# A new order of emission for a fused attention and gated convolution kernel on one core

## The chip, the core and the metric

The kernel runs on one core of a Trainium2 chip. The metric is the device time in microseconds (us) of one execution. TensorE (PE in the profile) multiplies matrices, with its weight loads shown as PEld; VectorE is DVE, ScalarE is ACT, GpSimd is POOL, SyncE is SP, which here only starts transfers.

## The reference, cut to what matters

For each of 8 batches `x` is 8 heads x 512 rows x 64, and `state` 8 heads x 32 rows x 64. The rows of `x` and the rows of `state` read each other by softmax attention, and what both read goes, as 544 rows of 512 features, through a gated convolution network:

```python
scores = scale * np.matmul(x, state.transpose(0, 1, 3, 2))       # softmax over the 32 state rows -> a
xread = np.matmul(a, state)
scores2 = scale * np.matmul(state, x.transpose(0, 1, 3, 2))      # softmax over the 512 rows -> a2
sread = np.matmul(a2, x)
h = np.maximum(x @ w_in, 0.0)                                    # x: xread and sread, heads side by side
conv_out += conv_w[k][None, None, :] * hp[:, k:k + S, :]         # 3 taps along the rows
gate = 1.0 / (1.0 + np.exp(-conv_out))
return (h * gate @ w_out).astype(np.float32)
```

## The kernel before

The kernel is one program of some 1,660 small operations. Each is recorded by `add(engine, kind, function, reads, writes)` and has a number by the place at which it was recorded. `Plan.order` then emits them in the order of the list `ORDER`: a number is an operation, `-n` puts n filling multiplications (`fill`, L215, on tile `idle`, whose result nobody reads) on PE, and a `v` behind a number puts an operation that ACT does by default onto DVE. Each engine, and each queue of transfers, takes its operations in the order in which the list gives them; waits are made from the data and the buffers. So the list is the schedule, and nothing else decides it. Eight PSUM banks (`PSUM = dict(ps=8)`) are handed round among all that PE writes.

What PE does, per batch b:

- **scores** (L310 into `ps_s`; for batch 0 in two halves, L320): 8 multiplications that use 64 rows and 32 columns of the array each.
- **flips** (L355 into `ps_t`, 4 transposes of 128 columns), **reads** (L368 into `ps_r`, 32 multiplications on 32 columns each), and **read flips** (L379 into `ps_f`, one transpose): the state rows' own softmax and what they read.
- **state products** (L548 into `ps_u`, for half hf of the hidden features; for batch 0 in blocks of 1, 1, 2 and 4 times 128 features, L567): state times `w_in`, 8 multiplications of the same shape as the scores. ACT and DVE split the result into two parts, `u0` (high) and `u1` (low).
- **hidden** (L630 into `ps_h`, 6 multiplications of 128x128 by 512 columns each; batch 0 has 4 of 256 columns, L637) and **projections** (L705 into `acc`, 3 multiplications of 512 columns for each of 4 row groups c and 8 feature blocks f; the very first ones L713).
- **state tokens** (L615 into `ps_hs`, 4 of 128 columns) and their projection (`acc_t`), and at the end of batch 0 one leftover projection (`acc_c`).

I call L630, L637, L705 and L713 the wide multiplications and all the others small groups. Batch 0's softmax over the state rows is done with PE's help: flip of the scores (L488 into `ps_x`), maximum (DVE, L492), shift (L498 into `ps_s`), exponential (ACT, L508 into `p`), sum (L512), reciprocal (DVE), spread (L498 into `ps_x`), division (DVE, L523), all in two halves q.

Between hidden and projection stand, for each of 64 steps, a relu on ACT (L200, or DVE), a first tap on ACT (L194), two taps on DVE (L673, L678), tanh on ACT (L682), the gate on DVE (L687), and a split into a high part (ACT, L205) and a low part (DVE, L208). The weights come as raw words and are rounded on the way in by ACT (L243 into `hc`, L246) and DVE (L249, L252, L260). All large loads stand in SP's queue; ACT's queue holds the first part of the state (`st`, the part of batch 0) and the convolution's weights.

Names that the change and the prediction use: tile numbers behind a name tell copies apart, and `e` is the exponential of a score half (L346), which the flips read.

Of the kernel before, what the change touches and what calls it, by code (L numbers as in the profile page):

```python
# [58 lines left out]
0 98 99 100 101 102 103 120 -9 123 121 125 -3 124 -1 142 143 126 2 -2 150 3 127 5 20 4 144 151 128 6 -1 152 132 145  # L59
146 130 7 21 461 14 23 15 17 22 147 16 148 24 18 25 153 19 154 155 133 8 9 462 10 135 11 149 32 467 33 463 12 156 34  # L60
468 469 26 489 28 136 27 530 35 1 13 36 129 464 157 29 37 38 131 189 30 465 466 39 190 40 41 531 532 31 192 42 200 534
199 191 43 515 490 44 535 491 45 47 193 46 202 203 48 205 516 493 204 517 49 536 206 502 503 210 504 519v 494 537 520
211 122 137 212 470 471 472 538 521 159 158 208 161 213 506 545 575 546 138 162 214 163 134 507 560 207 56 50 51 139
209 169 495 140 201 215 52 170 533 496 576 590 164 179 53 508 54 497 141 172 55 165 180 522 216 62 57 59 217 167 64 63
65 539 66 523 67 591 547 166 168 173 518 58 218 561 500 219 562 240 241 509 243 60 160 510 171 174 499 244 61 501 246
514 513 505 512 524 525 540 245 526 251 175 108 247 176 252 177 249 254 181 109 529 528 74 68 69 178 70 563 255 511 71
182 72 297 298 541 300 250 73 183 242 256 110 111 527 549 548 301 592 542 543 248 544 550 253 257 338 339 75 258 577
551 259 184 552 260 185 553 564 579 302 341 342 492 343 565 77 186 76 78 580 566 291 281 289 285 187 286 290 555 86 80
421 567 282 82 287 295 581 188 556 296 81 292 568 87 83 283 582 595 288 569 84 79 380 379 89 583 293 85 554 88 112 593
612 113 92 642 613 284 578 616 596 498 597 657 614 627 114 643 628 557 294 194 631 598 570 629 197 382 195 106 617 90  # L70
115 599 571 91 594 1516 558 559 574 572 573 198 196 349 600 618 116 1654 585 584 586 104 93 383 95 646 94 117 107 96
1655 658 660 619 615 645 620 97 647 601 384 118 1656 602 1657 119 105 672 717 687 589 588 702 621 644 1658 673 703 648
632 587 649 603 604 606 608 609 420 605 630 1659 650 235 230 633 236 634 659 350 233 1660 220 238 610 635 221 622 636
718 651 705 674 688 222 352 624 625 704 223 353 661 231 239 234 237 637 423 626 640 224 225 652 226 655 641 227 232
228 662 607 611 229 639 706 691 690 656 623 638 1661 721 676v 663 654 707 677 664 665 424 678 666 340 425 719 689 692
667 708 679 693 722 426 694 695 755 740 741 709 756 758 696 710 261 653 770 670 815 669 671 720 680 845 711 846 681
427 675 800 785 697 390 682 684 685 385 757 743 759 700 771 686 668 774 344 683 723 744 724 760 712 761 698 699 725
713 849 772 745 345 762 726 773 786 775 763 764 742 347 715 816 348 727 262 746 714 747 729 776 777 734 728 263 765
789 264 730 830 778 748 701 735 1662 831 788 749 819 817 716 732 801 733 265 271 328 346 850 266 790 272 351 354 847
# [874 lines left out]
```

## Time and profile before

| what | value |
| --- | --- |
| time, median of 3 runs | 356.75 us (355.89 to 357.86) |
| span of the profiled execution | 354.1 us |
| PE busy, share of the span | 348.6 us, 98% |
| DVE busy | 316.1 us, 89% |
| ACT busy | 256.1 us, 72% |
| granted TensorE clock | 1.00 |
| HBM read and written | 25.71 MB and 8.91 MB |

The profiled execution's own time is not listed apart from its span; the median of the timed runs lies 2.65 us above the span. The page's 40 slices show PE at 90% or more from the second slice (8.9 us) on, DVE at 90% or more in the slices 2 to 25 (to about 221 us) and less behind them, and ACT at 90% or more up to some 70 us. A row of the timeline gives the start of a run of like instructions, its busy time, engine, line, tiles, shape and count; a multiplication of 32-bit floats is counted twice, one of the split parts (512 columns, L630 and L705) once. The busy times of neighbours overlap, so what a group costs is read from its start to the next start.

### The profile page before, as it was taken

What the parts mean: (1) busy time and instruction counts of PE and PEld (TensorE: products, weight loads), DVE (VectorE), ACT (ScalarE), POOL (GpSimd) and SP (SyncE); (2) the same over time, 40 slices, a digit from 0 to 9 for tenths busy, and PEclk for the clock granted to TensorE, in tenths of its full rate; (3) what the DMA queues carried; (4) which work ended last, traced back from release to release, by engine and by line L of the source; (5) the groups of instructions that cost most, each with busy time, mean ns of one, the idle gap of its engine ahead of it and who ended that gap; (6) DMA issues with size and microseconds to landing.
All of it is one profiled execution on the core that took longest, in us unless ns stands there. A gap on an engine that the chain in (4) does not pass through costs nothing.

```text
span 354.1 us, 6694 instructions
## 1 busy us (share of the span) xinstructions
PE 348.6 (98%) x2538; PEld 271.8 (77%) x2538; DVE 316.1 (89%) x563; ACT 256.1 (72%) x560; POOL 29.4 (8%) x90
## 2 busy tenths in 40 slices
PE   7999999999999999999999999999999999999995
PEld 6766758876788868878789887878788868888884
DVE  1999999999999999999999999987799898889950
ACT  3999999998777997859856657774745447548642
POOL 1000000010000000100000300042201001113000
PEclk9999999999999999999999999999999999999999
DMA  7989998201600033030400000001200011000205
GB/s 255 396 309 377 328 357 302 62 1 50 219 0 2 0 127 142 3 119 32 180 30 2 0 31 31 30 3 60 89 2 0 0 71 65 2 2 0 74 33 176
DMA packets 13584, 35.06 MB, mean 99 GB/s; under 512 B 1520, under 2 KB 4720, under 8 KB 12528
## 3 DMA queue, kind: packets, MB, share of 16 engines
q1 hardware_dynamic: 12976, 34.28, 27.1%
q8 instruction: 20, 0.33, 0.4%
q10 hardware_dynamic: 576, 0.35, 0.3%
q14 instruction: 12, 0.10, 0.1%
HBM read 25.71 MB, written 8.91 MB: 98 GB/s over the span
## 4 chain that ended last, share of the span: by engine, by line
PE 97%; DMA 2%; ACT 0%; SPq 0%; issue 0%
PE acc L705 47%; PE ps_h L630 22%; PE ps_h L637 4%; PE ps_hs L615 4%; PE ps_u L548 4%; PE acc_t L705 3%; PE ps_r L368 2%; PE ps_t L355 2%; PE ps_s L310 2%; DMA xt<-xT 2%; PE acc_c L705 2%; PE acc L713 2%; PE ps_u L567 1%; PE ps_s L498 1%; PE ps_x L498 1%; PE ps_x L512 1%
## 5 line engine op out<-in xcount | busy, mean ns | idle before, releaser
L705 PE MATMUL acc<-wo,g 128*128 128x512 f32 x726 | 177.0, 393 | 0.0
L705 PEld LDWEIGHTS acc<-wo,g 128*128 128x128 f32 x726 | 134.7, 188 | 32.8 <-issue 1.7
L630 PE MATMUL ps_h<-a,u 128*128 128x512 f32 x336 | 83.2, 391 | 0.0
L630 PEld LDWEIGHTS ps_h<-a,u 128*128 128x128 f32 x336 | 62.7, 188 | 13.1
L682 ACT ACTIVATE t<-t 128x512 f32<-128x512 f32 x64 | 39.9, 630 | 14.5 <-DVE t L678 14.3
L673 DVE SCALAR_TENSOR_TENSOR t<-h,cw,t 128x511 f32<-128x511 f32 x64 | 47.1, 742 | 1.6 <-ACT t L194 1.5
L678 DVE SCALAR_TENSOR_TENSOR t<-h,cw,t 128x512 f32<-128x512 f32 (+1 forms) x64 | 46.8, 745 | 0.6
L205 ACT ACTIVATE g<-t 128x512 fp32r<-128x512 f32 (+1 forms) x62 | 37.5, 615 | 11.0 <-DVE t L687 5.5
L687 DVE SCALAR_TENSOR_TENSOR t<-t,h 128x512 f32<-128x512 f32 (+1 forms) x64 | 42.4, 667 | 2.3 <-ACT t L682 2.2
L208 DVE TENSOR_TENSOR g<-t,g 128x512 fp32r<-128x512 f32 (+1 forms) x62 | 41.3, 671 | 3.5 <-ACT g L205 3.1
L194 ACT ACTIVATE t<-h,cw 128x512 f32<-128x512 f32 x52 | 36.9, 723 | 4.3 <-DVE h L202 3.0
L200 ACT ACTIVATE h<-ps_h 128x512 f32<-128x512 f32 x56 | 33.3, 596 | 9.3 <-PE ps_h L630 6.1
L648 POOL COPY h<-hs 128x1 f32<-128x1 f32 x40 | 14.2, 376 | 129.2 <-ACT sr L383 66.3
L205 ACT ACTIVATE u<-ps_u 128x512 fp32r<-128x512 f32 x28 | 16.2, 596 | 8.5 <-PE ps_u L548 8.5
L719 ACT ACTIVATE o<-acc 128x512 f32<-128x512 f32 (+1 forms) x30 | 15.8, 544 | 8.5 <-PE acc L705 8.3
L648 POOL COPY hs<-h 128x1 f32<-128x1 f32 x40 | 13.6, 361 | 97.6 <-ACT h L200 80.9
L208 DVE TENSOR_TENSOR u<-ps_u,u 128x512 fp32r<-128x512 f32 x28 | 18.6, 682 | 2.5 <-ACT u L205 2.5
L615 PEld LDWEIGHTS ps_hs<-sr,wi 128*128 128x128 f32 x128 | 14.8, 192 | 1.1 <-ACT t L194 0.8
L637 PE MATMUL ps_h<-p,u 128*128 128x256 f32 x64 | 15.3, 386 | 0.0
L615 PE MATMUL ps_hs<-sr,wi 128*128 128x128 f32 x128 | 15.0, 276 | 0.0
L548 PE MATMUL ps_u<-wi,st 64*32 64x512 f32 x224 | 14.3, 597 | 0.0
L637 PEld LDWEIGHTS ps_h<-p,u 128*128 128x128 f32 x64 | 11.6, 190 | 3.3 <-DVE hc L249 0.8
(99 smaller groups left out, 400.3 us busy)
## 6 DMA issues: line engine op xcount, KB each, us to landing
xt<-xT SPq DMA_DIRECT2D x16, 512.0 KB, 7.7
xx<-xn SPq DMA_DIRECT2D x8, 1024.0 KB, 5.9
out<-o SPq DMA_DIRECT2D x27, 256.0 KB, 2.1
raw<-w_in SPq DMA_DIRECT2D x8, 512.0 KB, 7.6
raw<-w_out SPq DMA_DIRECT2D x8, 512.0 KB, 7.4
out<-o SPq DMA_DIRECT2D x6, 128.0 KB, 1.8
out<-o_t SPq DMA_DIRECT2D x8, 64.0 KB, 1.7
st<-stT SPq DMA_DIRECT2D x1, 448.0 KB, 10.2
```

The source lines that it names most:

```text
L194: A.activation(dst, src, AF.Copy, scale=scale)
L200: A.activation(dst, src, AF.Relu, scale=0.5)
L205: A.activation(hi, src, AF.Copy)
L208: engine.tensor_tensor(lo, src, hi.bitcast(F32), op=ALU.subtract)
L615: PE.matmul(ps_hs[m, f][:, :NT], wi[:, k, f * P:(f + 1) * P], sr[m][:, k, :], start=(k == 0), stop=(k == NK - 1))
L630: PE.matmul(ps_h[i], u[j][:, g, fs], a[k][:, g, :], start=(n == 0), stop=(n == 3 * NG - 1))
L637: PE.matmul(ps_h[f][:, q * HS:(q + 1) * HS], us[0, f // 4][0][:, g, f % 4 * P:(f % 4 + 1) * P], half_of(pa[0], q)[:, g, :], start=(g == 0) ...
L673: V.scalar_tensor_tensor(t[:, 1:], h[:, :S - 1], cw[:, f, 0:1], t[:, 1:], op0=ALU.mult, op1=ALU.add)
L678: V.scalar_tensor_tensor(t[:, :n], h[:, 1:n + 1], cw[:, f, 2:3], t[:, :n], op0=ALU.mult, op1=ALU.add)
L682: A.activation(tt[i], tt[i], AF.Tanh, scale=0.25)
L687: V.scalar_tensor_tensor(tt[i][:, :n], tt[i][:, :n], 1.0, hd[i][:, :n], op0=ALU.add, op1=ALU.mult)
L705: PE.matmul(acc, g[j][:, cs], wo[:, k, f, :], start=(f == 0 and n == 0), stop=(f == NF - 1 and n == 2))
```

## The change

Only the list `ORDER` is another one: the same operations, in another order. Both lists hold 16 fills: before, 9, 3, 1, 2 and 1 in the first microseconds; now 7, 3, 1, 1, 1 and 1 there and two single ones among batch 0's hidden products. By a `v`, DVE takes 25 operations before and 24 now: 12 and then 11 first taps (L196), 8 and then 7 relus (L202), and 5 evacuations of sums at the end (L721; four of 512 columns, one of 256) and then 6 (one of 512, five of 256). One line of the list, before and now:

```diff
@@ ORDER
-0 98 99 100 101 102 103 120 -9 123 121 125 -3 124 -1 142 143 126 2 -2 150 3 127 5 20 4 144 151 128 6 -1 152 132 145
+0 98 99 100 -2 101 -3 102 103 -2 120 123 125 -1 121 -2 142 2 124 126 3 143 144 145 14 -1 127 132 5 150 151 -1 4 146 6
...
```

In ACT's queue the first part of the state is the first transfer in both orders. In SP's queue the rest of the state (`st`, L894) stands 9th before and 11th now, with one load of `x` and one of `w_in` more ahead of it.

The first place is PE in the first microseconds, batch 0's softmax by PE (`ps_x` the flipped scores and later the spread sums, `ps_s` the scores that are shifted, `heads` the sum). Before, the two flips stand ahead of both shifts:

```order
L488 MATMUL ps_x_141<-ident,at_112 128x128 x4
L215 MATMUL idle<-zeros 128x128 x2
L488 MATMUL ps_x_154<-ident,at_112 128x128 x4
L498 MATMUL ps_s_0_0_113<-eight,m_0_146 32x128 x8
L498 MATMUL ps_s_0_1_114<-eight,m_0_146 32x128 x8
L215 MATMUL idle<-zeros 128x128
L498 MATMUL ps_s_1_0_130<-eight,m_1_183 32x128 x8
L498 MATMUL ps_s_1_1_131<-eight,m_1_183 32x128 x8
L512 MATMUL ps_x_141<-heads,p_208 128x4 x4
L355 MATMUL ps_t_215<-ident,e_0_185 128x128 x4
```

Now, on the same engine, behind the first flip (which has moved ahead of the second half of the scores, the eight L321 rows just before these):

```order
L499 MATMUL ps_s_0_0_111<-eight,m_0_149 32x128 x8
L499 MATMUL ps_s_0_1_112<-eight,m_0_149 32x128 x8
L216 MATMUL idle<-zeros 128x128
L489 MATMUL ps_x_178<-ident,at_110 128x128 x4
L216 MATMUL idle<-zeros 128x128
L513 MATMUL ps_x_128<-heads,p_167 128x4 x4
L499 MATMUL ps_s_1_0_135<-eight,m_1_183 32x128 x8
L499 MATMUL ps_s_1_1_136<-eight,m_1_183 32x128 x8
L499 MATMUL ps_x_128<-ident,s_0_211 32x128 x16
L216 MATMUL idle<-zeros 128x128
```

The first half's flip, shift and sum have moved ahead of the second half's; the flip of `e_0` has moved behind the spread.

The second place is PE among batch 0's hidden products (`ps_h`, each `x2` is one half). Before, behind the second batch's scores (last row of them first):

```order
L310 MATMUL ps_s_1_412<-xt_388,st 32x512
L637 MATMUL ps_h_396<-p_208,u_0_223 128x256 x2
L637 MATMUL ps_h_438<-p_208,u_0_223 128x256 x4
L368 MATMUL ps_r_457<-xx_455,e2t_359 32x64 x16
L368 MATMUL ps_r_457<-xx_455,e2t_331 32x64 x16
L567 MATMUL ps_u_3_0_493<-wi,st 32x512
```

Now, at the same place:

```order
L311 MATMUL ps_s_1_393<-xt_312,st 32x512
L638 MATMUL ps_h_344<-p_167,u_0_241 128x256 x2
L638 MATMUL ps_h_429<-p_167,u_0_241 128x256 x4
L216 MATMUL idle<-zeros 128x128
L638 MATMUL ps_h_447<-p_167,u_0_241 128x256 x4
L369 MATMUL ps_r_464<-xx_445,e2t_347 32x64 x16
L369 MATMUL ps_r_464<-xx_445,e2t_342 32x64 x16
L568 MATMUL ps_u_3_0_500<-wi,st 32x512
```

Four products more stand behind the scores, and a fill between them; a second such fill stands 23 rows further on.

The third place is PE and DVE where batch 2's projections begin (`ps_t` the flips of batch 7, `acc` the sums). PE before, from the last row of a state product on; the second flip stands alone among wide multiplications 48 rows further on:

```order
L548 MATMUL ps_u_0_1_1683<-wi,st 32x512
L368 MATMUL ps_r_1701<-xx_1424,e2t_1607 32x64 x16
L368 MATMUL ps_r_1701<-xx_1424,e2t_1339 32x64 x16
L355 MATMUL ps_t_1740<-ident,e_14_1508 128x128 x4
L705 MATMUL acc_3_1358<-wo,g_15_1586 128x512
```

PE now, from the last two rows of a state product on, which itself follows the read:

```order
L549 MATMUL ps_u_0_0_1727<-wi,st 32x512
L549 MATMUL ps_u_0_1_1728<-wi,st 32x512
L356 MATMUL ps_t_1744<-ident,e_14_1721 128x128 x4
L356 MATMUL ps_t_1764<-ident,e_15_1673 128x128 x4
L706 MATMUL acc_1_1328<-wo,g_15_1607 128x512
L706 MATMUL acc_1_1328<-wo,g_15_1606 128x512 x2
```

DVE before, around the low half of a state product (`u1`) whose bank the sum `acc_3` of batch 2 takes over:

```order
L454 TENSOR_TENSOR af_3_1463<-af_3_1463,s1_3_1666 128x1024
L678 SCALAR_TENSOR_TENSOR t_23_1577<-h_23_1503,cw_78,t_23_1577 128x512
L457 STREAM_TRANSPOSE at_3_737<-af_3_1463 128x1024
L208 TENSOR_TENSOR g1_18_1750<-t_18_1553,g0_18_1749 128x512
L208 TENSOR_TENSOR u1_3_0_1669<-ps_u_3_0_0_1670,u0_3_0_1668 128x512
L673 SCALAR_TENSOR_TENSOR t_21_1655<-h_21_1605,cw_78,t_21_1655 128x511
```

DVE now, around the low half whose bank `acc_3` takes over in the new order:

```order
L458 STREAM_TRANSPOSE at_3_683<-af_3_1533 128x1024
L674 SCALAR_TENSOR_TENSOR t_20_1717<-h_20_1481,cw_78,t_20_1717 128x511
L197 TENSOR_SCALAR t_22_1761<-h_22_1660,cw_78 128x512
L209 TENSOR_TENSOR u1_4_0_1726<-ps_u_4_0_1_1728,u0_4_0_1725 128x512
L209 TENSOR_TENSOR a1_3_1759<-at_3_683,a0_3_1758 128x1024
```

The read, the state product and both flips stand in one stretch now, and the bank comes from another state product, that of batch 4, which stands 231st on DVE; the one before stood 229th.

## Rows read from the trace of the kernel before

**Rows 1.** The page, sections 1 and 4: busy time by engine; the chain's shares.

```profile
PE 348.6 (98%) x2538; PEld 271.8 (77%) x2538; DVE 316.1 (89%) x563; ACT 256.1 (72%) x560; POOL 29.4 (8%) x90
...
PE 97%; DMA 2%; ACT 0%; SPq 0%; issue 0%
```

**Rows 2.** Busy time by engine in a stretch; stretch, length, engines, clock, DMA share, GB/s.

```profile
20.00:140.00 120.00, 119.96 (x1040) 88.83 (x1040) 117.64 (x207) 106.19 (x247) 2.40 (x4) 1.00 0.46 163
```

**Rows 3.** Timeline of PE, a lone state product; start, busy us, engine, line, what, count.

```profile
233.53 2.88 PE L705 MATMUL acc<-wo,g 128*128 128x512 f32 x12
236.34 1.09 PE L548 MATMUL ps_u<-wi,st 64*32 64x512 f32 x16
237.36 5.07 PE L705 MATMUL acc<-wo,g 128*128 128x512 f32 x21
242.27 2.88 PE L630 MATMUL ps_h<-a,u 128*128 128x512 f32 x12
244.99 0.84 PE L705 MATMUL acc<-wo,g 128*128 128x512 f32 x3
```

**Rows 4.** Timeline of PE, two state products side by side.

```profile
287.05 1.52 PE L705 MATMUL acc_t<-wo,gts 128*128 128x512 f32 x6
288.50 1.95 PE L548 MATMUL ps_u<-wi,st 64*32 64x512 f32 x32
290.38 2.33 PE L705 MATMUL acc<-wo,g 128*128 128x512 f32 x9
292.55 1.52 PE L630 MATMUL ps_h<-a,u 128*128 128x512 f32 x6
```

**Rows 5.** Timeline of PE, a lone flip, and a flip right behind a read.

```profile
120.97 0.60 PE L355 MATMUL ps_t<-ident,e 128*128 128x128 f32 x4
121.32 3.70 PE L705 MATMUL acc<-wo,g 128*128 128x512 f32 x15
124.85 1.52 PE L630 MATMUL ps_h<-a,u 128*128 128x512 f32 x6
...
130.57 0.66 PE L355 MATMUL ps_t<-ident,e 128*128 128x128 f32 x4
130.99 7.09 PE L705 MATMUL acc<-wo,g 128*128 128x512 f32 x30
137.92 0.27 PE L379 MATMUL ps_f<-ident,rr 128*128 128x128 f32 x1
```

**Rows 6.** Timeline of all engines in the first 24 us, the softmax of batch 0.

```profile
1.03 3.70 PE L215 MATMUL idle<-zeros 128*128 128x128 f32 x18 [1.03 <-DVE zeros L177]
...
5.81 0.66 ACT L194 ACTIVATE at<-ps_s 128x256 f32<-128x256 f32 x2 [0.76 <-PE ps_s L320]
...
8.09 0.60 PE L488 MATMUL ps_x<-ident,at 128*128 128x128 f32 x4
...
9.57 1.08 PE L498 MATMUL ps_s<-eight,m 128*32 128x128 f32 x32
...
10.05 0.72 ACT L346 ACTIVATE e<-at,nm 128x512 f32<-128x512 f32 x1 [0.17 <-DVE nm L340]
...
13.57 0.69 ACT L508 ACTIVATE p<-ps_s 128x256 f32<-128x256 f32 x2
...
16.36 0.77 PE L567 MATMUL ps_u<-wi,st 64*32 64x256 f32 x16
...
18.07 1.99 PE L637 MATMUL ps_h<-p,u 128*128 128x256 f32 x8
...
19.99 0.45 PE L567 MATMUL ps_u<-wi,st 64*32 64x128 f32 x16
```

**Rows 7.** The transfer of the rest of the state: its issue; size and time to landing.

```profile
6.53 0.43 SPq L894 DMA_DIRECT2D st<-stT  x1
...
st<-stT SPq DMA_DIRECT2D x1, 448.0 KB, 10.2
```

**Rows 8.** Timeline of DVE, the low half of a state product (`u1_3_0`).

```profile
134.10 0.68 DVE L208 TENSOR_TENSOR u<-ps_u,u 128x512 fp32r<-128x512 f32 x1
```

More of the change, by code (lines that the diff above doesn't have):

```diff
@@ new lines @@
+829 844 859 321 322 309 310 889 828 843 902 958 873 323 856 874 959 875 440 960 395 311 312 903 961 324 325 860 392
+1521 441 1522 922 357 358 876 923 396 842 857 858 307 326 928 890 299 891 929 930 877 739 973 943 944 945 886 313 333
+397 398 314 315 931 904 866 867 905 974 976 946 975 316 317 327 1041 962v 963 399 442 443 473 444 487 477 474 892 478
[5 rows of a table added]
+994 995 1034 359 969 984 1020 1057v 1059 408 1021 360 361 1089 1104 1060 1005 1035 1006 1071 1072 369 372 410 411 373
+370 371 1036 481 482 483 1527 1528 362 1010 1025 1040 412 1009 1050 1007 1022 1075 363 364 1037 1051 1052 365 1074 366
@@ new lines @@
+1105 1076 1529 1008 1023 1038 1061 413 367 368 1106 1058 484 1062 1090 1024 1039 988 1073 1077 1078 989 1091 414 1054
+1063 1530 1079 1124 1125v 1080 1055 1064 1154 1065 1139 1066 999 1053 1092 1107 1093 1094 1169 1170 1081 1069 1070
+1140 1143v 1095 1096 1108 1068 1109 374 1141 1127 409 377 378 1085 1155 1171 1084 1083 1110 1173 1099 1111 375 376
+1098 1113 1100 1174 1175 1176 1532 1128v 1158 1129 1533 1229 1126 1130 1199 1144 1131 1067 1534 1535 1536 1537 1132
+1133 1538 1159 1145 1082 1177 1230 1115 1122 1232 1146 1147 1097 1156 1112 1116 1117 1540 1160 1161 1114 1134 1184
@@ new lines @@
+1178 1162 1163 1541 1542 1543 1531 1539 1118v 1185 1214 1179 1148 1136 1149 1142 1157 1135 1150 1172 1544 1164 1151
+415 1215 1218 1217 1188v 1189 1186 1166 1216 1187 1200v 1201 1119 1138 1137 1153 1168 1545 1152 1546 416 1167 1182
+1219 1190 1548 1120 1549 1550 1203 418 419 1204 1551 1165 1552 1252 449 1191 1192 1205 1206 1207 1180 417 1193 1194
+1183 1220 1357 1312 1221 1222 450 1197 1253v 1553 1554 1208 1282 1358 1198 1209 1359 1202 1256 1231 1212 1313 1223
+1315 1556 1254 1257 1258 1557 1547 1558 1283v 1286v 1195 1181 1196 1255 1224 1285 1233 1259 1210 1316 1317 1287 1260
[4 rows of a table added]
@@ new lines @@
+1306 1307 1571 1264 1380 1381 1279 1263 1265 1280 1410 1576 1577 1578 1292 1585 1383 1346v 1347 1396 1579 1398 1294
+1281 1348 1296 1349 1278 1293 1364 1329 1308 1586 1587 1350 1588 1589 1590 1591 1365 458 1295 1331 1332 1333 1351 1352
+1592 1399 1321 1322 1311 1326 1580 1584 1583 1309 1411v 1582 1414v 1366 1581 1593 1310 1397 1324 1594 1595 1323 1325
+1425 1334 1335 1596 1597 1413 1598 1599 1336 1337 1341 1382 1384v 1385 1601 1386 1387 1485 1340 1400 1401 1602 1426
+1603 1455 1429 1430 1427 1604 1249 1339 1605 1606 1607 1338 1353 1367 1431 1609 1388 1389 1415 1610 1368 1354 1440
@@ L121 @@
+1412 1355 1372 1373 1402 1600 1456v 1459 1390 1428 1611 1612 1416 1369 1356 1371 1457 1417 1370 1460 1403 1404 1405
[4 rows of a table added]
+1634 1635 1636 1637 1638 1639 1484 1641 1642 1488 1643 1644 1645 1481 1646 1647 1499 1512v 1513 1496 1500 1502v 1503
+1640 1648 1649 1650 1652 1514v 1651 1501 1452 1467 1653 1482 1515 1497 1504v 1506v 1507 1505 1468 1483 1498 1508 1510
+1511 1509
 """
```

25 lines of the change are left out of this document (3 added, 22 removed), and 74 rows, old and new, of the table ORDER.

## The prediction

> **What bounds the kernel now.** I read the busy shares and the chain of waits first: PE is busy 348.6 of 354.1 us and holds 97% of the chain that ends last [rows 1]. Then the stretches: from 20 to 140 us PE has 119.96 of 120 us, so it waits for nothing there, at a granted clock of 1.00 (the 2.4 GHz level); but DVE has 117.64 of the same 120 [rows 2], so it runs with 2.36 us in hand. Behind some 220 us DVE is freer. So the time is the sum of what PE is given, plus a head of some 7 us before it is fed. A new order adds and removes no product. It can pay in three ways only: by the changes between kinds of multiplication, by an earlier first product, and by waits that it makes or spares. None has much to give.
>
> **The change part by part.** *Joins.* I price a group by starts: from the start of what stands before it to the start of what stands behind, less the wide multiplications at their own price. That price is (244.99 − 242.27)/12 = 0.2267 us [rows 3]. A lone state product: 242.27 − 233.53 = 8.74, less 33 × 0.2267 = 7.48, is 1.26 [rows 3]. Two side by side: 292.55 − 287.05 = 5.50, less 15 × 0.2267 = 3.40, is 2.10 [rows 4]. So two together save 2 × 1.26 − 2.10 = 0.42. A lone flip costs 124.85 − 120.97 = 3.88, less 15 × 0.2267 = 3.40, that is 0.48. A flip behind a read: 137.92 − 130.57 = 7.35, less 30 × 0.2267 = 6.80, is 0.55 [rows 5]; of this 0.15 belongs to the next entry into a small group (the 21 wide ones before 242.27 took 4.91 instead of 4.76 [rows 3]), which leaves 0.40. So a flip joined to a read saves 0.08, a fifth of the other.
>
> In the two orders, from the first hidden product on, small groups stand in 34 separate stretches among wide multiplications before and in 22 now (the two stretches that hold only a fill not counted). The places at which one small group touches another rise from 23 to 36. Of these 13 more, two are 64-row groups beside 64-row groups (state products, scores: 6 before, 8 now), none is a 64-row group beside a read (6 and 6), and 11 are of flips, read flips or state tokens (11 and 22). Dear joins: 2 × 0.42 = 0.84. The cheap ones lie between 0 (a read flip is one transpose, a quarter of a flip) and 0.08 each; I take 0.05, since over half are flips: 11 × 0.05 = 0.55. Sum 1.39, bounds 0.84 and 1.72. PE is the bound, so all of it counts.
>
> The rows show where the price sits: the lone state product goes 236.34 to 237.36, 1.02; the two together 288.50 to 290.38, 1.88 [rows 3, 4]. The second costs 0.86, so 0.16 is saved inside, and the rest at entry. The Trainium skill, "TensorEngine Tiling (Array Packing)", section Key Properties, says that changing the tiling mode, not just the tile, drains the engine. By that page only joins of one mode would pay, and the sum would be 0.84 instead of 1.39. The flip behind a read is of another mode, and 0.08 was saved, so the trace agrees only in part.
>
> *Fills among the hidden products.* Two of the 16 stand there now. Nine of them at the start take 3.70 (18 in the row, since each counts twice), so one is 3.70/9 = 0.41 us [rows 6]. If PE would not wait at that place, it is lost: 2 × 0.41 = 0.82. If it would wait there anyway, nothing. I take 0.82: PE did not wait there before.
>
> *The head.* Before, the flip of the first scores starts at 8.09 and its shift at 9.57, 1.48 later; the scores' copies on ACT end at 5.81 + 0.66 = 6.47 already, and between stand the second half's scores [rows 6]. Now this flip stands ahead of those, so the first half's chain can start some 1.5 us earlier. The second half still waits for its own scores, and on ACT the exponential `e` (10.05, 0.72 and 0.17 of wait), which stood ahead of the second half's `p` (13.57), now stands behind it [rows 6]: that takes 0.72 + 0.17 = 0.89 off ACT's chain to `p`. The flips of `e` stand behind and then wait some 0.2 for it, so the first hidden product (18.07) comes 0.7 earlier; bounds 0 (`p` not on the path) and 0.89. But by then a block of 128 features has been multiplied in place of the one of 256: 0.77 − 0.45 = 0.32 is only put off [rows 6]. Net 0.70 − 0.32 = 0.38, bounds −0.32 and 0.57.
>
> *The state's load.* The first part of the state is first in ACT's queue in both orders, so there the words of the change say nothing new. The rest of the state goes back in SP's queue by two loads of 512 KB. It was issued at 6.53 and landed 10.2 later, at 16.7 [rows 7]; its first use stands behind the 128 block, at 19.99 + 0.45 = 20.4 [rows 6]. With eight loads ahead of it these 10.2 make 10.2/9 = 1.1 for each place in the queue, so two places more are an estimated 2.3, and it lands at 19.0. That is ahead of its use by 1.4, so I take nothing; each further microsecond would hold up the next state product and all that follows. The loads that it lets pass come earlier, and PE waits for none of them at that time.
>
> *Places on DVE.* One first tap and one relu go back to ACT, which has room behind 70 us. The evacuations at the end are the same in kind: I take nothing. What the order does to DVE's due times is the open cost. At the first multiplication of batch 2's `acc_3`, in the run of 30 that starts at 130.99, PE needs a bank that the low half `u1_3_0` empties on DVE at 134.10 + 0.68 = 134.78 [rows 8]. In this run it is the 19th: 130.99 + 18 × 0.2267 = 135.07 [rows 5], so 0.3 of slack. Now it needs the low half of batch 4, 231st on DVE instead of 229th, while 314 wide multiplications instead of 323 are ahead of it on PE: PE comes 9 × 0.2267 = 2.04 earlier and DVE two instructions of about 0.68 later, 1.36. If DVE has no more in hand than before, PE waits 2.04 + 1.36 − 0.3 = 3.1 there; if the small groups ahead of it differ, or the 2.36 us of DVE's idle time [rows 2] lie ahead of it and close, 3.1 − 2.36 = 0.7, or nothing. A wait that is once paid moves PE back against DVE for all that follows, so such waits do not add up. I take 0.3, since before PE waited nowhere in that stretch; bounds 0 and 3.1.
>
> Sum: 1.39 − 0.82 + 0.38 − 0.30 = 0.65 faster. The span goes from 354.1 to 353.4. The median of the runs lies 2.65 above the span, so the time goes from 356.75 to **356.1**.
>
> **The rivals.** *DVE sets the pace (slower).* The place is the one above. For it: 98% of DVE's time is taken between 20 and 140 us, and nine products fewer stand ahead of the bank. Against it: PE never waited there before, and a list that puts small groups together gives DVE its inputs in larger lots, which may also come earlier. The price is 2 to 4 us of PE waits in place of the 0.3: time 356.75 − 0.95 + 2 to 4 = 357.8 to 359.8. It makes the kernel slower once the waits exceed the gain of 0.95, and measurably so from 0.95 + 1.78 = 2.7 on.
>
> *Joins of different kinds save nothing.* Then only the two dear joins pay: 0.84 − 0.82 + 0.38 = 0.40, time 356.35. For it: a read flip is a single transpose, and its place may be too short to save anything. Against it: the 0.08 of the flip behind a read, though that is a difference of two readings of 3.9 and 7.4 us. The rule on modes in the page named above would give this time.
>
> *All that is open falls well.* PE would wait at the fills anyway, the cheap joins are worth 0.08 and the head gives 0.57: 1.72 + 0.57 = 2.29 and no waits, time 354.5. For it: with the small groups among batch 0's hidden products at other places, waits may be there that were not before, and a fill in one is free. Against it: PE waited nowhere behind 20 us, and two of the three bounds would have to be met at once.
>
> *The order does not do what it says.* The joins are there in the list, but the state's load comes later than its first use, and the state product behind the 128 block waits with all behind it. A delay of 1 to 2 us beyond the 1.4 in hand gives 357.1 to 358.1. Against it: eight loads ahead took no more than 10.2 together.
>
> **How the numbers follow.** Forecast (DVE's waits below 1 us) 0.51; DVE sets the pace 0.20; joins of one kind only 0.12; all falls well 0.13; the load late 0.04. Two timings of this kernel can be told apart from about 0.5%, 1.78 us: faster is below 354.97, slower above 358.53. Faster holds most of the case in which all falls well and a little of the forecast, by the median's own scatter (355.89 to 357.86): 0.12 + 0.07 = 0.19. Slower holds some 0.6 of DVE's case and a little of the load's: 0.12 + 0.01 = 0.13. Same: 0.68. For 8 in 10 I leave out the upper part of DVE's case (0.11) and the lower part of the gain (0.08): 354.7 to 358.2.
>
> **What would show it.** *Joins:* two state products side by side cost 2.1 between their neighbours' starts, and PE's busy time falls by about 1.4 with fills and head apart. A flip joined to a read at 0.5 says that the cheap joins are nothing. *Fills:* a unit of 0.41 between hidden products with no wait beside it; a wait right behind it says that it cost nothing. *Head:* `p` of the second half some 0.9 and the first hidden product some 0.7 earlier, at 17.4; if not, `p` was not on the path. *State:* landing before 20 us. *DVE:* no idle time of PE put down to DVE between 20 and 140 us, at `acc_3` of batch 2 above all; 2 us or more of it there makes the forecast wrong on the slow side, and one large wait on the load or on ACT would do so too. A time below 354.9 would say that a join is worth about twice what I read.

## The result and the profile after

The changed kernel takes 359.49 us, median of 14 runs, against 356.78 us of 14 runs of the kernel before: a ratio of 1.0067, 95% interval 1.0048 to 1.0085. That is slower by 0.7%, outside the forecast range of 354.7 to 358.2 and on the other side of no change. One execution, the one that was profiled with the result, ran PE at half its pace to the end (708.61 us, span 706.8) and does not count in the ratio (median of the other 13: 359.24), so the profile shown here is of another execution of the same kernel, of 357.52 us, shorter than all of those 13 (358.21 to 360.62).

In every run that lists both, the time lies 1.8 us above the span (357.52 and 355.7 here). So the profile of the kernel before, with its span of 354.1, is that of its run of 355.89, the shortest of the three, and the 2.65 us of the forecast are these 1.8 and the 0.9 from that run to the median. The two profiles differ by 1.6 us of the 2.5 by which the medians differ.

First the page and the stretch from 20 to 140 us, as in [rows 1, 2]:

```profile
PE 348.4 (98%) x2538; PEld 272.3 (77%) x2538; DVE 318.8 (90%) x562; ACT 258.5 (73%) x561; POOL 30.7 (9%) x90
...
PE 66%; DVE 22%; ACT 5%; DMA 4%; issue 2%; SPq 0%; DVEq 0%; ACTq 0%
```

```profile
20.00:140.00 120.00, 118.97 (x1040) 88.47 (x1039) 118.07 (x208) 107.79 (x252) 0.78 (x2) 1.00 0.41 148
```

PE's busy time is the same to 0.2 us, but its share of the chain has fallen from 97% to 66%, and DVE has taken 22%. From 20 to 140 us PE now stands still for 1.03 us where it stood still for 0.04. What PE waited for (engine, tile and line, what it waited for; us in all, times, longest):

```profile
PE ps_s L321 <- DMA xt<-xT: 0.9, 1, 0.9
PE ps_r L369 <- DMA xx<-xn: 0.5, 1, 0.5
PE acc_t L706 <- DVE gts L209: 0.4, 1, 0.4
PE acc L706 <- DVE u L209: 0.4, 1, 0.4
```

The last three have no like in the profile of the kernel before: the load of `x` for a read, the last state tokens' gates, and the low half of a state product (`u`), which is the place of the forecast's slower rival. The wait for a load of `x` does appear in other profiles of the order of before: 0.4 us with seven fills, and 0.9 in the relieved kernel before (both below). The head, to be read against [rows 6]:

```profile
1.03 3.35 PE L216 MATMUL idle<-zeros 128*128 128x128 f32 x14 [1.03 <-DVE zeros L178]
5.26 0.67 PE L321 MATMUL ps_s<-xt,st 64*32 64x256 f32 x16 [0.87 <-DMA xt<-xT]
5.86 0.94 PE L216 MATMUL idle<-zeros 128*128 128x128 f32 x6
6.63 0.60 PE L489 MATMUL ps_x<-ident,at 128*128 128x128 f32 x4
...
12.72 1.00 SPq L895 DMA_DIRECT2D st<-stT  x1
...
12.88 0.63 ACT L509 ACTIVATE p<-ps_s 128x256 f32<-128x256 f32 x2
...
17.70 2.76 PE L638 MATMUL ps_h<-p,u 128*128 128x256 f32 x12
```

The first flip stands at 6.63 instead of 8.09, the second `p` at 12.88 instead of 13.57, the first hidden product at 17.70 instead of 18.07.

To say where time goes I use three marks that both kernels share: the start of the first, the 121st and the last (1210th) hidden product or projection, taken from the starts of single multiplications in each trace.

| profile | first | first to 121st | 121st to last |
| --- | --- | --- | --- |
| kernel before | 18.07 | 52.55 | 279.53 |
| changed kernel | 17.70 | 53.27 | 280.92 |
| without two fills | 19.36 | 53.46 | 280.95 |
| nine fills at the start | 17.84 | 53.64 | 280.85 |
| before, seven fills | 17.84 | 53.18 | 279.53 |
| three waits mended | 18.46 | 54.53 | 279.56 |
| two waits mended | 17.94 | 55.54 | 279.49 |
| relieved, after | 21.00 | 52.31 | 279.53 |
| relieved, before | 18.25 | 54.92 | 279.52 |
| reads earlier | 20.97 | 54.60 | 279.55 |
| head of before | 18.43 | 56.08 | 279.48 |
| head of after, before | 20.22 | 53.15 | 279.53 |
| fewer loads, after | 18.12 | 52.62 | 279.47 |
| fewer loads, before | 19.69 | 52.33 | 279.51 |

(The names are those of the experiments below; the kernels put together from two lists at 41 and 72 us and the joins alone are not listed; "before" behind a comma is the kernel before with that edit.) The last column repeats to 0.1 us from profile to profile, at 280.9 in the changed order and at 279.5 in the others; the first two do not. The second varies in the order of before as well (52.33 to 54.92), so a single profile says little there. The changed kernel loses 1.4 in the last, a varying amount in the second, and a varying amount ahead of the first product. Between the two orders only the second and third columns together hold like work: the new order has one state product more and a few state-token multiplications fewer ahead of its 121st product. Over both it has two fills more (0.44) and a block of 256 features in place of one of 128 (0.2).

### The profile page after: what moved, and what is told of

Its sections match the earlier page's. It is cut to its first block, busy times and chain, and to the rows that moved or that the text cites. A ratio compares the mean times of both kernels' runs of the same rounds, so it can differ in the third digit from the quotient of the medians.

```text
span 706.8 us, 6681 instructions
## 1 busy us (share of the span) xinstructions
PE 701.5 (99%) x2538; PEld 439.1 (62%) x2538; DVE 326.2 (46%) x562; ACT 263.7 (37%) x561; POOL 21.6 (3%) x90
## 4 chain that ended last, share of the span: by engine, by line
PE 99%; DMA 1%; issue 0%; ACT 0%
PE acc L706 48%; PE ps_h L631 22%; PE ps_hs L616 4%; PE ps_h L638 4%; PE ps_u L549 4%; PE acc_t L706 3%; PE ps_t L356 2%; PE ps_r L369 2%; PE ps_s L311 2%; PE acc L714 2%; PE acc_c L706 2%; DMA xt<-xT 1%; PE idle L216 1%; PE ps_u L568 1%; PE ps_s L499 1%; PE ps_x L499 1%
## 5 line engine op out<-in xcount | busy, mean ns | idle before, releaser
L706 PE MATMUL acc<-wo,g 128*128 128x512 f32 x726 | 354.4, 678 | 0.0
L706 PEld LDWEIGHTS acc<-wo,g 128*128 128x128 f32 x726 | 214.4, 297 | 124.5 <-issue 112.1
L631 PE MATMUL ps_h<-a,u 128*128 128x512 f32 x336 | 166.4, 675 | 0.0
L631 PEld LDWEIGHTS ps_h<-a,u 128*128 128x128 f32 x336 | 101.2, 302 | 56.1 <-issue 50.2
L616 PEld LDWEIGHTS ps_hs<-sr,wi 128*128 128x128 f32 x128 | 30.2, 347 | 6.3 <-DVE u L209 1.9
L638 PE MATMUL ps_h<-p,u 128*128 128x256 f32 x64 | 31.5, 685 | 0.0
L616 PE MATMUL ps_hs<-sr,wi 128*128 128x128 f32 x128 | 31.1, 446 | 0.0
L549 PE MATMUL ps_u<-wi,st 64*32 64x512 f32 x224 | 28.0, 1123 | 0.0
L638 PEld LDWEIGHTS ps_h<-p,u 128*128 128x128 f32 x64 | 19.1, 302 | 10.8 <-issue 10.0
L706 PE MATMUL acc_t<-wo,gts 128*128 128x512 f32 x48 | 25.2, 664 | 0.0
```

The costliest lines, as they stand in the source:

```text
L549: PE.matmul(ps_u[b, hf, g][j * NS:(j + 1) * NS, :], st[half, b * NP + j, :], wi[half, j, hf * 512:(hf + 1) * 512], start=True, stop=True)
L616: PE.matmul(ps_hs[m, f][:, :NT], wi[:, k, f * P:(f + 1) * P], sr[m][:, k, :], start=(k == 0), stop=(k == NK - 1))
L631: PE.matmul(ps_h[i], u[j][:, g, fs], a[k][:, g, :], start=(n == 0), stop=(n == 3 * NG - 1))
L638: PE.matmul(ps_h[f][:, q * HS:(q + 1) * HS], us[0, f // 4][0][:, g, f % 4 * P:(f % 4 + 1) * P], half_of(pa[0], q)[:, g, :], start=(g == 0) ...
L706: PE.matmul(acc, g[j][:, cs], wo[:, k, f, :], start=(f == 0 and n == 0), stop=(f == NF - 1 and n == 2))
```

## Experiments

All ratios below are against runs of the kernel before on the same chip.

**The changed kernel once more, and without the two fills.**

```diff
@@ ORDER (second kernel)
-212 -1 122
+212 122
...
-214 -1 508
+214 508
```

> The changed kernel once more, as it is, for a second profile. Theory (DVE sets the pace): PE idles or its runs stretch by 2 to 4 us between 20 and 140 us, first at acc_3 of batch 2, and DVE's idle time there falls or stays near 2.4 us. Rival (the joins give less and fills and head cost more): PE stays busy without a wait, and the price of the groups, summed from start to start, is about 2.5 us above that of the kernel before.

> The changed kernel without its two fills among batch 0's hidden products. If PE is the bound there: 0.8 us faster than the changed kernel (359.5 to 358.7). If PE would wait there in any case, or DVE sets the pace behind it: no difference, 359.5.

The first gave the profile above. The second: 359.18 us, ratio 1.0060 (1.0037 to 1.0084), no different from the changed kernel. Its stretch to the 121st product is 53.46 instead of 53.27: in these two profiles, two units of filling taken out of PE gave PE no time. The forecast's price of 0.82 was too high in any case: in the trace a unit there takes 0.22, not 0.41, which came from the slow first microseconds. A cost of 0.44 is within the intervals, so that PE's own work no longer sets the pace there is likely and not shown. The rival of the first expectation, PE without a wait, is out; its theory is met at the place and not in size, with 1.03 us of standstill instead of 2 to 4. But the second profile shows a head that the first did not:

```profile
1.03 3.35 PE L216 MATMUL idle<-zeros 128*128 128x128 f32 x14 [1.03 <-DVE zeros L178]
5.57 1.11 PE L321 MATMUL ps_s<-xt,st 64*32 64x256 f32 x16 [1.18 <-DMA xt<-xT]
6.61 1.65 PE L216 MATMUL idle<-zeros 128*128 128x128 f32 x6
8.05 1.06 PE L489 MATMUL ps_x<-ident,at 128*128 128x128 f32 x4
```

The same instructions took 0.67, 0.94 and 0.60 above. PE is still at half pace when the second scores start, and the first product comes at 19.36. In the kernel before, the nine units at the start [rows 6] ended at 4.73, and single starts in them go from 0.21 to 0.11 apart at 4.12. The seven units now end at 4.38, all 0.21 apart, and PE stands still for 0.87 to 1.18 before the scores.

**Nine fills in the changed kernel, seven in the kernel before.**

```diff
@@ ORDER (first kernel, from the changed one)
-98 99 100 -2 101 -3 102 103 -2 120
+98 99 100 -4 101 -3 102 103 -2 120
```

```diff
@@ ORDER (second kernel, from the one before)
-120 -9 123
+120 -7 123
```

> The changed kernel with nine fills instead of seven ahead of the first scores (the first -2 of the list is -4). Theory A (PE leaves its half pace only after enough unbroken work, and seven fills end just before that): the flips and scores of the first 10 us run at full pace in the profile, the first hidden product stands at 17.7 us or earlier as in the better of the two profiles, and the median falls from 359.4 by 0.5 to 1.0, to 358.4 to 358.9. Theory B (the pace at the start is chance, or does not matter): no difference, 359.4.

> The kernel before with seven fills instead of nine ahead of the first scores, and nothing else. Theory A: half pace lasts into the first flips in some executions, the median rises from 356.8 by 0.3 to 1.0. Theory B: the two fills lie in the wait for the first load, no difference, 356.8.

With nine fills the changed kernel takes 358.23 us, 1.0044 (1.0019 to 1.0070); the kernel before with seven takes 358.00, 1.0028 (1.0003 to 1.0052), with runs from 355.8 to 360.4. By the ratios both moved by 0.8 to 1.0 us in the direction of theory A; only the second is outside its interval. Why is not shown: the two profiles have their first product at 17.84, the changed kernel's stands at 17.70 and that of the kernel before at 18.07. Nor do nine always suffice: in 7 of 15 profiles with nine, PE was at half pace until 6.6 to 7.2 us. With seven it was once 8.7 us or more, and in the execution named above full pace did not come.

**Three waits mended.**

```diff
@@ ORDER (from the changed one, with nine fills)
-268 430 805 737 269 834v 332
+268 430 332 805 737 269 834v
...
-1503 1640 1648 1649 1650 1652 1514v 1651 1501 1452 1467 1653
+1503 1452 1467 1640 1648 1649 1650 1652 1514v 1651 1501 1653
...
-242 256 544 219 178 86 542 76 78 184 79 257 258 259 301 543 260
+242 544 256 219 178 86 542 76 78 184 79 257 258 301 543 259 260
```

> The changed kernel with nine fills at the start and with three waits of PE taken away by moves in the list: the last state tokens' projections stand behind six more products, the low half of batch 4's state product stands ahead of two taps on DVE, and the read of batch 3 stands behind three products. Theory C (the joins save what was forecast, and waits elsewhere eat it): each of the three waits (0.54 at 346, 0.52 at 134, 0.53 at 53 us) goes without a new one, and the body from the first hidden product to the last product is 1.5 shorter than in the changed kernel, 332.7 instead of 334.2; median 357.0 to 357.4. Theory D (DVE sets the pace through the body, so that a wait taken away comes back at the next bank): the body stays at 334.2 or within 0.5 of it; median as with the nine fills alone.

358.52 us, 1.0052 (1.0033 to 1.0071): no gain in the median, yet the profile splits. 121st to last is 279.56, down from 280.85: the waits at 134 and 346 us went and did not come back. The read moved behind three products was a loss: those products need a gate of DVE that came just as late as the load, and first to 121st grew to 54.53. So theory C held for two waits and theory D for the third; the body from first to last, 334.1, is the 334.2 of theory D.

**Two waits mended.** The same without the third move.

```diff
@@ ORDER (from the changed one, with nine fills)
-268 430 805 737 269 834v 332
+268 430 332 805 737 269 834v
...
-1503 1640 1648 1649 1650 1652 1514v 1651 1501 1452 1467 1653
+1503 1452 1467 1640 1648 1649 1650 1652 1514v 1651 1501 1653
```

> The changed kernel with nine fills and the two moves that took away the waits at 134 and 346 us; the read of batch 3 stays where the change put it. By the profiles so far the two moves are worth 0.68 and 0.69 us against the changed kernel with nine fills alone: median 356.8 to 357.2. If DVE sets the pace and a wait taken away only moves: 358.0 to 358.4.

358.04 us, 1.0032 (1.0011 to 1.0053), runs from 356.5 to 359.9. The expected 356.8 to 357.2 is missed, and the median is the rival's, but its mechanism is not seen: 121st to last is 279.49, so the two waits did not move elsewhere in it. PE in the changed kernel around the first of the two places (first fence) and in this one (second):

```profile
131.67 2.32 PE L706 MATMUL acc<-wo,g 128*128 128x512 f32 x9
134.35 3.02 PE L706 MATMUL acc<-wo,g 128*128 128x512 f32 x12 [0.36 <-DVE u L209]
```

```profile
134.16 5.04 PE L706 MATMUL acc<-wo,g 128*128 128x512 f32 x21
139.04 2.88 PE L631 MATMUL ps_h<-a,u 128*128 128x512 f32 x12
```

Nine products took 134.35 − 131.67 = 2.68, 0.64 more than 9 × 0.2267; the 21 together now take 4.88. DVE's low half, which ended at 134.78 in [rows 8], ends at 133.61 + 0.68 = 134.29 in the changed kernel, earlier, but PE is there earlier still:

```profile
133.61 0.68 DVE L209 TENSOR_TENSOR u<-ps_u,u 128x512 fp32r<-128x512 f32 x1
```

The other place, the last state tokens (changed kernel, then mended):

```profile
345.29 0.84 PE L706 MATMUL acc_t<-wo,gts 128*128 128x512 f32 x3
346.51 0.98 PE L706 MATMUL acc_t<-wo,gts 128*128 128x512 f32 x3 [0.38 <-DVE gts L209]
```

```profile
348.43 1.52 PE L706 MATMUL acc_t<-wo,gts 128*128 128x512 f32 x6
```

The first three take 1.22 to the next start instead of 0.68; mended, the six take 1.36. Of the 1.4 that PE saves, what follows the last product takes back 0.4 (4.29 to the span's end instead of 3.85). That the state tokens are stored later would explain it. PE's share of the chain goes with these two waits: it was 66% and is here, on the page of this profile, 93%:

```profile
PE 93%; DMA 5%; DVE 0%; issue 0%; ACT 0%; SPq 0%
```

And this profile shows what is left: PE waited 2.8 us for two loads of `x`.

```profile
PE ps_r L369 <- DMA xx<-xn: 2.8, 2, 1.8
```

**Halves of both lists put together.** In the first and third the list of the kernel before runs up to the place it reaches at 72 or at 41 us, and what is left follows in the changed order; the second is the reverse.

```diff
@@ ORDER (first kernel: from the one before)
 95 646 94 117 107
-96 1655
+644 647 630 235
...
@@ ORDER (second kernel: from the changed one)
 117 572 648 104 573
+614 594 1516 574
...
@@ ORDER (third kernel: from the one before)
 513 505 512 524 525
-540 245
+511 498 245 247
...
```

> The list of the kernel before up to the place that it reaches at some 72 us, and from there the remaining operations in the order of the changed kernel, with the two moves that took away the waits at 134 and 346 us (the low half of batch 4's state product earlier on DVE, the last state tokens' projections later). Theory E (what the joins save is small, some 0.5, and the loss lies in the first 70 us, where ACT and DVE are both full): the part behind 72 us costs 0.2 to 0.6 less than before, median 356.2 to 356.8. Theory F (the new order loses behind 70 us too): median 357.5 or more, with waits of PE for DVE behind 72 us.

> The reverse: the list of the changed kernel, with nine fills at the start, up to the same place, and from there the remaining operations in the order of the kernel before. Theory E: the loss of the first 70 us remains, about 1.1 us of the body, median 357.7 to 358.3. Theory F: about as the kernel before, 356.8 to 357.2.

> As the first of these, but the list of the kernel before only up to the place that it reaches at some 41 us. If the loss of the first 70 us arises ahead of 41 us, in the softmax of batch 0 and the hidden products with the fills: as the first of these, 356.2 to 356.8. If it arises between 41 and 70 us: 0.6 to 1.1 more, 357.2 to 357.7.

359.49 (1.0076), 358.35 (1.0044) and 358.23 us (1.0034). The first is slower than either half would suggest, but a joint, the place where the lists meet, makes waits of its own: from the state product behind it (79.23) to the next small group the first costs 2.54 beyond its wide products instead of the 1.26 of [rows 3], and in the second the stretch at the joint costs 1.5 more than the same groups elsewhere. Without these 1.5 the second would stand at 356.85, the median of the kernel before beside it, and the new first 72 us with nine fills would cost nothing. But a joint can also hide a wait, so these three do not decide between E and F.

**Relief of DVE and ACT.** The list with two waits mended and the kernel before, both with half the columns in three operations.

```diff
@@ before, behind, sigmoid (both kernels)
+        n = S // 2 if i < 24 else S
-        V.scalar_tensor_tensor(t[:, 1:], h[:, :S - 1], cw[:, f, 0:1], t[:, 1:], op0=ALU.mult, op1=ALU.add)
+        V.scalar_tensor_tensor(t[:, 1:n], h[:, :n - 1], cw[:, f, 0:1], t[:, 1:n], op0=ALU.mult, op1=ALU.add)
...
-        n = S if i >= NF else S - 1
+        n = S // 2 if i < 24 else S
...
-        A.activation(tt[i], tt[i], AF.Tanh, scale=0.25)
+        A.activation(tt[i][:, :n], tt[i][:, :n], AF.Tanh, scale=0.25)
```

> The same list, but DVE's two taps and ACT's tanh of the first 24 steps (batches 0 to 2) work on half their columns, which leaves part of the gates unfinished; PE's work and all waits are unchanged. It takes some 16 us from DVE and some 6 from ACT ahead of 150 us. Theory G (DVE and ACT hold PE up in the new order, and the joins save 0.5 to 1.4 on PE): the waits of PE between 20 and 140 us go, the median falls by 0.7 or more below the list without the relief, and it is 0.4 to 1.4 below the relieved kernel before. Theory H (the joins save nothing, the new order costs PE as much as the old): within 0.3 of the relieved kernel before, or above it.

> The kernel before with the same relief: half the columns in DVE's two taps and ACT's tanh of the first 24 steps. Theory G: PE waited for next to nothing there, so the gain is 0 to 0.5, median 356.3 to 356.8. If DVE held PE up in the kernel before as well, the gain is 1 or more.

357.51 us, 1.0029 (1.0007 to 1.0051), and 356.82 us, 0.9998 (0.9984 to 1.0012). DVE had 10.5 and 14.6 us in hand (first line: the new list; second: the kernel before):

```profile
20.00:140.00 120.00, 119.88 (x1047) 90.19 (x1047) 109.49 (x210) 103.34 (x252) 0.63 (x2) 1.00 0.42 150
```

```profile
20.00:140.00 120.00, 117.64 (x1029) 86.76 (x1028) 105.45 (x204) 101.25 (x244) 0.56 (x2) 1.00 0.46 163
```

The ratio of the new list went from 1.0032 to 1.0029, and of the kernel before not at all. Theory G, that DVE and ACT hold PE up all through this stretch, falls, though DVE did at the one bank. Two things in the profiles are against blaming the new order alone for what is left. The new list stands still for only 0.12 us here, with all its loads, and loses its time ahead of the first product, at 21.00. The relieved kernel before stands still for 2.36 us: PE waits 1.3 for ACT and 0.9 for a load of `x` ahead of two reads.

**Reads earlier, and joins alone.**

```diff
@@ ORDER (first kernel: from the list with two waits mended)
-522 241 209
+522 209
...
-518 575
+518 201 241 215 575
...
-547 512 66 247 68 69 160 174 577
+547 160 174 512 66 247 68 69 577
```

```diff
@@ ORDER (second kernel: from the one before; an operation, and behind or ahead of which it stands now)
+434 388
...
+393 306
...
+398 439
...
+374 415
```

> The list with nine fills and the two mended waits (the one measured at 358.04), with three moves around batch 0's end: one load of the transposed x stands behind the load of x for batch 2's read instead of ahead of it, batch 2's read stands one hidden product earlier, batch 1's read one projection earlier. x for the reads has one buffer, so each of these loads starts only when the read before it has ended. Theory I (what is left of the loss is PE's wait for these loads, 0.2 to 4.0 us in the profiles, longer or shorter from run to run): the waits fall below 0.5, the median to 357.3 or less and the spread of the runs to some 2 us. Theory J (it lies elsewhere): median 357.8 to 358.3.

> The kernel before with four joins behind 140 us and nothing else: two pairs of lone flips stand side by side (at some 148 and 163 us), a read flip stands behind another one, and the lone state product of 253 us stands beside that of 236 us. By the prices read: 0.42 for the state products, 0.1 for each of the others, so the stretches behind 140 us cost 0.7 less, if no wait arises; the median falls by 0.7, to 356.2, which the runs can hardly show. If joins save nothing on PE: the same cost. If a wait takes the place (a bank that is held longer, or DVE): the cost behind 140 us rises at the place of the join or at the next bank.

The first: 357.61 us, 1.0019 (0.9997 to 1.0040), some 0.4 better than without by the ratios, which is within the intervals; it is not down to the 357.3 of theory I. The second: 360.84 us, 1.0106 (1.0084 to 1.0128), 3.6 us slower for four joins. PE there:

```profile
168.56 0.65 PE L368 MATMUL ps_r<-xx,e2t 128*32 128x64 f32 x32 [0.27 <-ACT h L200]
169.76 0.65 PE L368 MATMUL ps_r<-xx,e2t 128*32 128x64 f32 x32 [0.55 <-ACT e2t L194]
...
239.12 1.09 PE L548 MATMUL ps_u<-wi,st 64*32 64x512 f32 x16
240.56 1.04 PE L548 MATMUL ps_u<-wi,st 64*32 64x512 f32 x2 [0.36 <-ACT h L200]
242.73 1.51 PE L548 MATMUL ps_u<-wi,st 64*32 64x512 f32 x14 [1.13 <-DVE u L208]
```

Two state products want four banks at once: from 239.12 to the next product at 244.17 they take 5.05 instead of the 1.88 of a pair without waits [rows 4], 3.2 more. And the second of two flips put later leaves its copy to ACT too late for the read.

**The first 20 us exchanged.** The last list with the first 20 us of the kernel before, and the reverse.

```diff
@@ ORDER (first kernel: from the one before)
 189 30 465 466 39
+200 134 490 502
...
@@ ORDER (second kernel: from the changed one, with nine fills)
 38 39 41 1 189
+468 469 530 129
...
```

> The last list (nine fills, two waits mended, reads earlier, measured at 357.61) with the first 20 us of the kernel before: its list up to the first products of batch 0, then the rest in the other order. Theory K (what is left of the loss is the changed order of batch 0's softmax: in two of six profiles the first hidden product came at 21 us, while it came at 17.8 to 19.0 in all with the order of before): 0.4 to 0.8 below that list, 356.8 to 357.2. If the head does not matter: 357.6.

> The reverse: the first 20 us of the changed list, with nine fills at the start, and from there the order of the kernel before. Theory K: 0.4 to 1.0 slower than the kernel before, 357.4 to 358.0, with some runs 2 to 3 us above the others. If the head does not matter: as the kernel before, 356.9 to 357.2.

357.82 us, 1.0017 (0.9999 to 1.0035), and 356.47 us, 0.9982 (0.9961 to 1.0002). Theory K falls: with nine fills the new head is no loss in either order (1.0019 and 1.0017 with and without it), and in front of the old order it gives the lowest ratio of all with the whole computation, though its interval still touches no difference.

**Fewer loads.** The list with two waits mended and the kernel before, with the loads of `x` for the reads of batches 1 to 3 left out.

```diff
@@ x_load (both kernels)
+        if 1 <= b <= 3:
+            xxs[b] = xxs[0]
+            return
         xxs[b] = buf([P, NCH, DM], F32, "xx", f"xx_{b}")
```

> The list with nine fills and the two mended waits (measured at 358.04), with the loads of x for the reads of batches 1 to 3 left out: those reads use batch 0's x instead, so the output of these batches is another one; every multiplication stays. It takes 3 of the 1 MB loads out of the first 60 us and all of PE's waits for them. Theory L (what is left of the loss between 20 and 70 us is PE's wait for loads in the new order): 0.8 or more below that list, 357.2 or less, and not above the kernel before with the same loads left out. Theory M (loads do not matter): 357.8 to 358.2, a microsecond above the kernel before so cut.

> The kernel before with the same three loads left out (the reads of batches 1 to 3 use batch 0's x). Theory L: it waits little for them, so 0 to 0.5 below the kernel before, 356.6 to 357.1. Theory M: 357.1.

356.72 us, 0.9999 (0.9980 to 1.0018), and 356.42 us, 0.9983 (0.9963 to 1.0002). By the ratios the new list gained 1.2 us by it and the old one 0.6. From 20 to 140 us (the new list, then the old):

```profile
20.00:140.00 120.00, 119.89 (x1046) 89.77 (x1045) 118.71 (x209) 108.20 (x252) 0.79 (x2) 1.00 0.35 122
```

```profile
20.00:140.00 120.00, 120.00 (x1041) 88.72 (x1040) 117.82 (x209) 106.99 (x249) 1.67 (x3) 1.00 0.39 139
```

PE's standstill of 3.06 us in the profile with two waits mended (116.94 of 120) is down to 0.11, and first to 121st from 55.54 to 52.62, the kernel before's 52.55. Theory L holds in that the new list gained more than 0.8 and came below 357.2. That it is not above the kernel before so cut (356.72 against 356.42) is within the intervals. The edit takes away three transfers with the waits for them, so it does not tell the wait for `x` from what those transfers do to others. DVE is fuller than in any other of these profiles, 118.71 of 120, and PE does not wait for it.

## Why the prediction was wrong

- **What bounds the kernel.** "PE is the bound, so all of it counts" is the step that failed. It was read from one order in one execution, in which PE met no wait behind 20 us. In the new order PE runs into two that are there in every profile, at 134 and 346 us: they cost 1.4 us behind the 121st product (280.9 against 279.5), of which 0.4 come back at the end, and with them PE's share of the chain is 65 to 71%. Moved out of the way, they are gone (279.5, 93%).
- **The start, priced at nothing.** The forecast listed seven fills in place of nine in the first run and gave the two no price, though it priced two fills elsewhere. In the runs they are worth some 0.8 and 1.0 us by the ratios (1.0067 to 1.0044, and 1.0028 for the kernel before with seven). Only the second is clear of its interval, which leaves room for 0.1 to 1.9.
- **The loads of `x` were not considered.** I looked only at the state's load. `x` for the reads has one buffer, so each of the loads starts when the read before it ends, and in most profiles of the new order PE comes to a read before its load is in. Without three of these loads the ratio falls from 1.0032 to 0.9999 (together the intervals leave room for a gain of 0.0005 to 0.0061), and the kernel before's from 1 to 0.9983; the difference, 0.0016 or some 0.6 us, would be what the new order lost there beyond the old. The intervals of all four leave room for 1.8 and for nothing, and the old order has such waits too in some executions. So that loads hold the new order up is shown, and that they do it more than in the old is not.
- **DVE at `acc_3`.** The place was right, and half of the mechanism: PE comes earlier, but DVE does not come 1.36 later; the low half that PE waits for ends 0.5 earlier than the one before (134.29 against 134.78). The price was taken as 0.3 with bounds of 0 and 3.1. It is 0.6 by the nine products above. As a rival I gave it 2 to 4 us and a chance of 0.20, as a wait that spreads; the 279.5 of the mended lists show that it stays at the one place.
- **The tail, taken at nothing.** Ahead of the last state tokens' projections PE waits 0.54 (1.22 − 0.68) for their gates' low half on DVE. The forecast looked only at the evacuations there.
- **The joins.** The price of a join of different kinds was right. A state product with a flip behind it, in the changed kernel:

```profile
112.74 2.88 PE L706 MATMUL acc<-wo,g 128*128 128x512 f32 x12
115.55 1.09 PE L549 MATMUL ps_u<-wi,st 64*32 64x512 f32 x16
116.57 0.66 PE L356 MATMUL ps_t<-ident,e 128*128 128x128 f32 x4
116.99 4.37 PE L706 MATMUL acc<-wo,g 128*128 128x512 f32 x18
121.20 1.52 PE L631 MATMUL ps_h<-a,u 128*128 128x512 f32 x6
```

  121.20 − 112.74 = 8.46, less 30 × 0.2267 = 6.80, is 1.66, against 1.26 + 0.48 = 1.74 apart [rows 3, 5]: 0.08 saved, as read for a flip behind a read. (The 0.15 that the prediction took off there as "the next entry into a small group" is misread: the 21 wide ones lead to other wide ones at 242.27, so it stands behind the state product.) The page that was named, the Trainium skill's "TensorEngine Tiling (Array Packing)", section Key Properties, ties the drain to a change of mode; the trace does not bear out that only joins of one mode save. But the sum of 1.39 is not there. In the two kernels with fewer loads PE next to never waits (0.11 and 0.00 us of standstill from 20 to 140 us). From the first to the last product the new list takes 332.09 and the old 331.84. Less the two fills (0.44) and the larger block (0.2), the new order saves 0.4, with whatever small waits it has; the relieved new list, 331.84, would make it 0.65. What became of the other half and more of the 1.39 is not shown. Four joins alone, in the kernel before, cost 3.6 us.
- **The fills among the hidden products**: forecast as a loss of 0.82, measured as none (359.18 against 359.49), with intervals that leave room for the 0.44 which the trace shows.
- **The head**: forecast 0.38 faster. The second half's `p` comes 0.69 earlier (0.89 was forecast) and the first product 0.37 (0.7 was). With nine fills in front of the old order it is 0.8 faster (356.47 against 357.28), with an interval from 1.4 to no gain; in front of the new order there is no difference (1.0019 against 1.0017). So the direction is not shown in the times.
- **The state's load**: issued at 12.72 and 7.4 us under way, it landed at 20.1 and not at 19.0; its first use there is the state product at 20.84, so nothing was lost, as said, by 0.7 instead of 1.4.

Added up as ratios: 1.0067 in all; nine fills bring it to 1.0044, and the two moves to 1.0032. From there earlier reads bring 1.0019, or three loads fewer 0.9999. Together nine fills, the two moves and the fewer loads take away 0.0068, clear of all intervals, and against the kernel before with the same loads left out 0.0016 stays, which is within them. So start, two waits and loads together hold the loss. Only the last step is larger than what its two intervals leave open, so neither the shares of the three nor their order of size is shown by the times; the two waits are shown by the traces.

## What to carry to other kernels

A kernel in which the profile shows one engine without a wait is not therefore free to move: its order is where the waits are not, and a new one must be held against every due time it changes, the single-buffered loads and the banks first. A join is worth what two neighbours save, a tenth of a microsecond here, and costs whatever its latest input brings; test it alone. Count filling work at the start as part of the schedule, with the execution it is needed in, not the one that was profiled. And look where the profiled execution lies among the timed ones, before a stretch without a wait is called a property of the kernel.

## What the runs showed of the hardware

PE's pace and the granted clock in the rows did not always agree. In the head of the kernel without the two fills, scores, fills and flips took 1.11, 1.65 and 1.06 instead of 0.67, 0.94 and 0.60, with single fills 0.21 us apart instead of 0.11, and in the half-paced execution all 706.8 us did, while the rows give a granted clock of 1.00 in both. The Trainium skill, "TensorE: Matmul & The Clock Gate", section "Seeing it yourself", warns that records of the gate are unreliable on this chip, and these two traces agree. In three of the profiles with the new head (relieved, reads earlier, head of after) PE fell back to that pace at 17 to 18 us, behind waits of 0.4 to 1.0, and the first product came at 20.2 to 21.0; two others waited 0.6 there and kept the pace. In these three the rows do show it: a granted clock of 0.50, the lower of the two levels (1.2 GHz), with single fills 0.21 apart as in the heads above. The stretch of the relieved new list from 15 us on and the next one:

```profile
15.00:20.00 5.00, 4.33 (x62) 3.40 (x63) 3.99 (x11) 5.00 (x14) 0.00 (x0) 0.76 1.02 410
20.00:25.00 5.00, 5.00 (x50) 3.77 (x57) 4.30 (x9) 3.85 (x9) 0.00 (x0) 0.89 1.02 417
```

So a recorded fall was a fall here, and a recorded 1.00 was no proof of full pace; starts of like instructions are the surer view.

A 1 MB load of `x` took 4.8 to 10.1 us from issue to landing in the first 60 us and 4.6 to 6.4 behind 80 us, where loads are few. Behind the 121st product equal work repeated to 0.1 us (279.47 to 279.56 in eleven profiles).
